# A fused attention and two-mixture kernel: the second mixture's relu is issued earlier in each step, and two integer additions change engine

## The chip, the cores and the metric

The kernel runs on one core of one Trainium2 chip. The metric is device time in microseconds (us) of one execution. Before the change the median of 3 runs is 1346.58 us (1345.78 to 1347.17).

## The reference

The input goes through three stages. Gated linear attention over 4 batches of 8 heads (768 positions, 48 columns) gives x, 3072 tokens of 384 columns. The first mixture ("moe") puts them through a hidden layer of 2048 with a rational gate, the second ("moe2") through four experts with a hidden layer of 1024 and a relu:

```python
def _moe_ref(x, w_in, w_out, a, b):
    h = x @ w_in
    h2 = h * h
    h3 = h2 * h
    P = a[0] + a[1] * h + a[2] * h2 + a[3] * h3
    Q = 1.0 + np.abs(b[0]) * np.abs(h) + np.abs(b[1]) * h2
    g = P / (Q + 1e-06)
    return (g @ w_out).astype(np.float32)

def _moe2_ref(x, domain_probs, w1, w2):
    N, D = x.shape
    E = w1.shape[0]
    p = domain_probs / (domain_probs.sum(-1, keepdims=True) + 1e-09)
    out = np.zeros((N, D), dtype=np.float32)
    for e in range(E):
        h = np.maximum(x @ w1[e], 0.0)
        out += p[:, e:e + 1] * (h @ w2[e])
    return out.astype(np.float32)
```

## The kernel before, in words

Sequence positions are cut into 6 chunks of 128; a chunk is 512 tokens (4 batches). Almost all products are done in a split form: an operand is kept as a rounded high part (gh, w's first half) and the remainder (gl, w's second half), and three products high·high, high·low, low·high are summed.

**Start (about 0 to 122 us).** `first` runs chunk 0's attention, batch by batch. Beside it `conv` turns the 16 weight slots of the first mixture from 64-bit words into 32-bit floats: two passes on ScalarE (L807, L808), a shift and a merge on VectorE (L810, L811), and an integer addition (L814). Slots 0 to 3 have that addition on VectorE, the other twelve on GpSimd. The slots then feed chunk 0's first mixture (`fill_in` L963, `fill_out` L971).

**Steps (from about 122 us).** The main loop has one step for each v of 192: chunk, expert and hidden tile of the second mixture, counted through. `product_order` fixes what TensorE does in a step, in this order: "in2" of tile v+1 (9 matmuls of 512 columns into a hidden bank, of which there are two, `hb[v % 2]`), "out2" of tile v-1 (9 matmuls), then in some steps "in1" of the next chunk's first mixture (9) and "out1" (36, the output of four gated tiles). Where a step has an "out1", tile v+2's "in2" is moved up into it. TensorE's attention matmuls are spread between these (scores L477, key transposes L493, outputs L501, state updates L544).

Beside TensorE a step does, in program order, which is the order in which ScalarE, VectorE and GpSimd take their instructions:

- `relu(v)`: ScalarE writes gh from the hidden bank (L1034), VectorE then writes gl from bank and gh (L1035). Until both have read the bank, "in2" of tile v+2 can't write it; "out2" of tile v needs both results.
- attention's exponentials and inverses (L431, L452), then `gate_in` and `gate_step`, the rational gate of one first-mixture tile: on ScalarE L980, L984 to L986, L1001, L1002 and L1011, on VectorE L995 to L1026. Inside it also stand the w pass of attention (L437) and `evac2`, which weighs an expert's finished sum with its probability (L1069) for GpSimd to add (L1076).
- the late operations of attention (`ops[REST]`): the scans (L444), newton2 (L468), q_hat (L473, GpSimd), the masks of the scores (L488), the copies L497 and L553, finish (L572).
- the splits of weights that are used for the first time (`split_to`): ScalarE rounds (L867), GpSimd, and VectorE in the first steps, subtracts (L869). `take` asks for these when a weight is used, and each step's end asks for up to four ahead.

`relu(v)` stands at the beginning of step v, behind all late operations and splits of step v-1. Only in steps with an "out1" is `relu(v + 1)` issued inside step v, behind the early "in2".

Of the kernel before, what the change touches and what calls it, by code (L numbers as in the profile page):

```python
# [17 lines left out]
NB, NH, S, D = 4, 8, 768, 48  # L18
# [319 lines left out]
CONV1 = (-5, -4, -3, -3, -1, 0, 1, 2, 3, 4, 5, 6, 7, 8, 9, 10)  # L338
NRAW = 8
PRE = 8  # L340
LAST = NCH * NE * NJ2
# [49 lines left out]
def where2(v):  # L391
    return v // (NE * NJ2), v // NJ2 % NE, v % NJ2
# [362 lines left out]
def fused(ctx, tc, aps, consts, gm, big, dp, prep, flag_op):  # L755


    nc = tc.nc
# [38 lines left out]
    def conv(i, stage):  # L797
        if stage == 0:
            t = spare_pools[i % 3].tile([128, 2 * SW], F32, tag=("o", "s1", "pb")[i % 3], name="t")
            temp[i] = t  # L800
        f = temp[i]
        p, m = f[:, 0:SW], f[:, SW:2 * SW].bitcast(I32)
        pi = p.bitcast(I32)
        words = raw[i].rearrange("p (n w) -> p n w", w=2)
        lo, hi = words[:, :, 0], words[:, :, 1]
        if stage == 0:
            nc.scalar.activation(out=p, in_=hi.bitcast(F32), func=AF.Abs, scale=2.0 ** -112, accum_out=big[:, i:i + 1])  # L807
            nc.scalar.activation(out=m, in_=lo.bitcast(U32), func=AF.Identity, scale=2.0 ** -29)  # L808
        else:
            nc.vector.tensor_scalar(pi, pi, 3, None, ALU.logical_shift_left)  # L810
            nc.vector.scalar_tensor_tensor(out=pi, in0=hi, scalar=-2 ** 31, in1=pi, op0=ALU.bitwise_and, op1=ALU.bitwise_or)  # L811
            w1f[i] = wp.tile([128, SW], F32, tag="w", name="wf")
            eng = nc.vector if CONV1[i] < NB - 6 else nc.gpsimd
            eng.tensor_tensor(out=w1f[i].bitcast(I32), in0=pi, in1=m, op=ALU.add)  # L814
            late.append(partial(nc.sync.dma_start, out=w1s[i], in_=w1f[i]))
            if i % 2:
                late.append(fetch)
# [68 lines left out]
    x2, hps, act1, act2 = {}, {}, {}, {}  # L886
# [10 lines left out]
    def fill_step():  # L897
        if fill["done"] < len(fill["ops"]):
            fill["i"] += 1
            to = len(fill["ops"]) * fill["i"]  # L900
            to = -(-to // fill["n"]) if fill["ceil"] else to // fill["n"]
            while fill["done"] < to:
                fill["done"] += 1
                fill["ops"][fill["done"] - 1]()

    def mm_in(ps, w, x):
        wh, wl = w
        n = 0
        for kk in range(3):
            o = slice(kk * 128, (kk + 1) * 128)  # L910
            for a, b in ((wh, x[:, 0]), (wh, x[:, 1]), (wl, x[:, 0])):
                nc.tensor.matmul(ps, a[:, o], b[:, kk, :], start=(n == 0), stop=(n == 8))  # L912
                n += 1
                fill_step()
# [19 lines left out]
    def run_bounds(v):  # L934

        return (v % NJ2 == 0 or v in groups), ((v + 1) % NJ2 == 0 or v + 1 in groups)

    def emit(item):
        kind, what = item
        ts = take(len(halves(item)))  # L940
        if kind == "pre":
            pass
        elif kind == "in2":
            c = where2(what)[0]
            mm_in(hb[what % 2], ts[0], x2[c])
        elif kind == "in1":
            c, j = what
            mm_in(h1, ts[0], att.x[c])
            gate_queue.append((c, j, h1))
        elif kind == "out2":  # L950
            if what >= LAST - NJ2:
                mm_tokens(ts[0], act2.pop(what), *run_bounds(what))
            else:
                mm_out([(ts[0], act2.pop(what))], *run_bounds(what))
        else:
            c, n = what
            mm_out([(ts[i], act1.pop((c, 4 * n + i))) for i in range(4)], True, True)
        make_ready(state["used"] + R)
# [12 lines left out]
            nc.tensor.matmul(acc[m], w[:, o:o + 128], g, start=(j == 0), stop=(j == NJ1 - 1))  # L971


    gate_queue, gate = [], {}

    def gate_in(u):
        h = u[2]
# [11 lines left out]
    def gate_step(new, old, ops):  # L989
# [34 lines left out]
        if old and old[0]:  # L1024
            gl = g1p.tile([128, 512], F32R, tag="gl", name="gl")
            vec.tensor_tensor(out=gl, in0=q0, in1=gh.bitcast(F32), op=ALU.subtract)  # L1026
            act1[old[:2]] = (gh, gl)


    def relu(v):  # L1030
        h = hb[v % 2]
        gh = g2p.tile([128, 512], F32R, tag="gh", name="gh")
        gl = g2p.tile([128, 512], F32R, tag="gl", name="gl")
        nc.scalar.activation(out=gh, in_=h, func=AF.Relu)  # L1034
        nc.vector.scalar_tensor_tensor(out=gl, in0=h, scalar=0.0, in1=gh.bitcast(F32), op0=ALU.max, op1=ALU.subtract)  # L1035
        act2[v] = (gh, gl)
# [85 lines left out]
    for v in range(-FILL - 6, LAST + 1):  # L1122
        tau = v + FILL
        state["vec"] = -1 <= v < 9
        ops = att.begin(v)
        if tau == -3:
            prep.load()
        if tau == -1:
            prep()
        if tau + 6 <= NB:  # L1130
            att.first(tau + 6, conv_ops(tau), fetch, partial(fill_in, 0, 0, NB - 1))
        run_late()
        store_all()
        items = steps.get(v, [])
        lead = 1 if items and items[0][0] == "in2" and items[0][1] == v + 1 else 0
        fill_run(ops[PA], 9 * lead)
        for item in items[:lead]:
            emit(item)
        if 0 <= v < LAST and v not in act2:
            relu(v)  # L1140
        while sums:
            sums.pop()()
        for f in ops[ACT0]:
            f()
        for u in gate_queue:
            if u[0] and u[:2] not in gate:
                gate[u[:2]] = gate_in(u)
        if 0 <= tau + 1 < NJ1:
            fill_in(tau + 1, (NB - 1) * (tau < 0))
        def outputs():  # L1150
            fill_run(ops[PB], 9 * any(item[0] == "out2" for item in items), True)
            for item in items[lead:]:
                if item[0] == "out2":
                    emit(item)
                    if run_bounds(v - 1)[1]:
                        evac2(v - 1)

        amid = 0 < v < LAST and run_bounds(v - 1)[1]
        if v - 1 in groups and groups[v - 1][1]:
            ops[ACT1].append(partial(evac1, *groups[v - 1]))  # L1160
        if amid:
            ops[ACT1].append(outputs)
        ready = [u for u in gate_queue if u[:2] in gate]
        new = ready[0] if ready else None
        if new:
            gate_queue.remove(new)
        old, pend_old = pend_old, new
        if new or old:
            gate_step(new, old, ops)
        else:  # L1170
            for f in ops[DVE1] + ops[ACT1] + ops[POOL1]:
                f()
        c, k = v // (NE * NJ2) - 1, v % (NE * NJ2)
        if v in (LAST - 4, LAST - 3):
            for b in range(2):
                write_out(NCH - 1, b + 2 * (v - LAST + 4), banks[6 + b])
        if 0 <= c < NCH - 1 and k == 2:
            for b in range(2):
                write_out(c, b + (2 if c else 0), banks[6 + b])
        if not amid:  # L1180
            outputs()
        for item in items[lead:]:
            if item[0] == "in2":
                emit(item)
                if v + 1 < LAST:
                    relu(v + 1)
        if 0 <= c < NCH - 1 and k == (1 if c else 2):
            for b in range(2):
                write_out(c, b + (0 if c else 2), banks[6 + b])
        for kind in ("pre", "in1", "out1"):  # L1190
            for item in items[lead:]:
                if item[0] == kind:
                    emit(item)
        for u in gate_queue:
            if not u[0] and u[:2] not in gate:
                gate[u[:2]] = gate_in(u)
        if tau == 0:
            spread_probs()
        if 0 <= tau < NB:
            att.blocks[0, tau].scale_state()  # L1200
        if 0 <= tau - 2 < NJ1:
            fill_out(tau - 2)
        for f in ops[REST]:
            f()
        if v in groups and not groups[v][1]:
            evac1(*groups[v])
        if tau + 6 > NB:
            for f in sum(conv_ops(tau), []):
                f()
            run_late()  # L1210
        if 10 <= tau and v < -1:
            make_ready(min(R - 6, 2 * (tau - 9)))
            split_to(min(AHEAD, state["ready"] - 2))
        if tau == NJ1 + 1:
            for m in range(3):
                split_x2(0, m, acc[m], nc.vector)
            load_pb(0)
        for f in ops[POST]:
            f()
        if v >= -1:  # L1220
            split_to(min(state["used"] + AHEAD, state["split"] + 4))
        att.loads(v)
        if v == 170:
            flag_op(banks[6], banks[7])
# [180 lines left out]
```

## Time and profile before

| | us |
|---|---|
| median of 3 runs | 1346.58 |
| profiled execution, its own time | 1346.18 |
| its span (first to last instruction) | 1344.30 |
| TensorE matmuls busy | 1321.2 |
| TensorE weight loads busy | 1058.5 |
| VectorE busy | 888.9 |
| ScalarE busy | 682.1 |
| GpSimd busy | 277.4 |

The mean granted TensorE clock is 0.999 of full speed. Engines run side by side, so the busy times don't add up to the span. A matmul's end in the profile is modelled, and consecutive matmuls overlap; where one engine waits, the row of the instruction behind the wait says so in brackets, with the instruction that ended it.

### The profile page before, as it was taken

Reading aid. Unit: us, or ns where it says so; the run is one execution under the profiler, and the core shown is the slowest. Engines: PE = TensorE matmul, PEld = TensorE weight load, DVE = VectorE, ACT = ScalarE, POOL = GpSimd, SP = SyncE. Lnnn points to the kernel's source line nnn. Section 1 sums busy time; section 2 is a strip of 40 time slices with the busy share of each in tenths; the row PEclk is TensorE's granted clock in tenths of the full one; section 3 lists DMA queues with packets and bytes.
Section 4 is the critical chain, followed back from the end, with each engine's and each line's share of the span. In section 5 each row is a group of like instructions: output and inputs, shape, how many; then the busy total and the mean of one; then the engine's idle time right before and its main releaser. Section 6 shows DMA issues by size and latency. Waiting matters only on the chain.

```text
span 1344.3 us, 19607 instructions
## 1 busy us (share of the span) xinstructions
PE 1321.2 (98%) x7180; PEld 1058.5 (79%) x7180; DVE 888.9 (66%) x1366; ACT 682.1 (51%) x1188; POOL 277.4 (21%) x234
## 2 busy tenths in 40 slices
PE   8999999999999999999999999999999999999998
PEld 8445888777788888888888888888888888888887
DVE  7998868998566666767575847575756565752221
ACT  6997568767265545345554525554525444421111
POOL 2333344576410022101020220010210010110010
PEclk9999999999999999999999999999999999999999
DMA  9538985777785666676666657656757666667660
GB/s 344 212 143 308 377 316 200 276 246 269 273 273 187 190 199 188 186 260 200 200 216 186 207 189 251 213 186 199 227 175 240 194 191 196 191 192 242 196 189 27
DMA packets 116856, 294.17 MB, mean 219 GB/s; under 512 B 13232, under 2 KB 28944, under 8 KB 115984
## 3 DMA queue, kind: packets, MB, share of 16 engines
q1 hardware_dynamic: 116320, 292.70, 65.7%
q8 instruction: 59, 0.97, 0.3%
q14 instruction: 45, 0.37, 0.1%
q10 hardware_dynamic: 432, 0.13, 0.0%
HBM read 243.98 MB, written 48.81 MB: 218 GB/s over the span
## 4 chain that ended last, share of the span: by engine, by line


## 5 line engine op out<-in xcount | busy, mean ns | idle before, releaser
L912 PE MATMUL bank<-x,w 128*128 128x512 f32 x2448 | 593.3, 391 | 6.3 <-DVE gl L1035 5.5
L912 PEld LDWEIGHTS bank<-x,w 128*128 128x128 f32 x2448 | 457.1, 188 | 103.3 <-DVE gl L1035 6.9
L922 PE MATMUL bank<-gh,w 128*128 128x512 f32 x1584 | 492.7, 392 | 2.0 <-ACT gh L1011 1.2
L922 PEld LDWEIGHTS bank<-gh,w 128*128 128x128 f32 x1584 | 294.0, 188 | 67.9 <-issue 4.0
L922 PE MATMUL bank<-gl,w 128*128 128x512 f32 x792 | 308.6, 390 | 0.0
L1035 DVE SCALAR_TENSOR_TENSOR gl<-bank,gh 128x512 fp32r<-128x512 f32 x192 | 131.7, 686 | 137.6 <-ACT gh L1034 137.2
L1076 POOL TENSOR_TENSOR o<-o,t 128x512 f32<-128x512 f32 x64 | 92.4, 1470 | 534.7 <-DVE t L1069 534.7
L1034 ACT ACTIVATE gh<-bank 128x512 fp32r<-128x512 f32 x192 | 113.7, 593 | 120.0 <-PE bank L912 120.0
L922 PEld LDWEIGHTS bank<-gl,w 128*128 128x128 f32 x792 | 148.7, 188 | 31.2
L1000 DVE SCALAR_TENSOR_TENSOR q<-q,sc,r 128x512 f32<-128x512 f32 x80 | 63.4, 793 | 142.3 <-ACT r L985 142.3
L1011 ACT CAST gh<-q 128x512 fp32r<-128x512 f32 x80 | 49.2, 615 | 163.0 <-DVE q L1009 162.8
L980 ACT COPY h<-bank 128x512 f32<-128x512 f32 x80 | 47.0, 588 | 117.5 <-PE bank L912 117.4
L1026 DVE TENSOR_TENSOR gl<-q,gh 128x512 fp32r<-128x512 f32 x80 | 58.3, 729 | 51.7 <-ACT gh L1011 51.7
L869 POOL TENSOR_TENSOR w<-rawbuf,w 128x384 fp32r<-128x384 f32 x68 | 80.1, 1204 | 32.2 <-ACT w L867 25.0
L1021 DVE SCALAR_TENSOR_TENSOR y<-y,sc,h 128x512 f32<-128x512 f32 x80 | 74.8, 935 | 2.8
L1001 ACT ACTIVATE r<-q,sc 128x512 f32<-128x512 f32 x80 | 58.0, 725 | 23.2 <-DVE q L1000 16.3
L995 DVE SCALAR_TENSOR_TENSOR q<-q,r 128x512 f32<-128x512 f32 x80 | 69.2, 864 | 0.1
L458 POOL TENSOR_TENSOR k<-k,g 112x512 f32<-112x512 f32 x23 | 34.4, 1498 | 156.3 <-DVE g L444 93.3
L986 ACT ACTIVATE y<-h,sc 128x512 f32<-128x512 f32 x80 | 64.2, 802 | 0.0
L1009 DVE SCALAR_TENSOR_TENSOR q<-y,sc,q 128x512 f32<-128x512 f32 x80 | 62.2, 778 | 1.8
L1093 DVE TENSOR_TENSOR s<-s,bank 128x512 f32<-128x512 f32 x45 | 30.0, 684 | 49.4 <-PE bank L922 49.4
L1002 ACT ACTIVATE r<-r 128x512 f32<-128x512 f32 x96 | 60.7, 633 | 3.0
(117 smaller groups left out, 1273.3 us busy)
## 6 DMA issues: line engine op xcount, KB each, us to landing
w<-ws SPq DMA_DIRECT2D x456, 384.0 KB, 3.5
ws<-w SPq DMA_DIRECT2D x96, 384.0 KB, 5.1
raw<-in_w_dram SPq DMA_DIRECT2D x16, 768.0 KB, 6.9
rawbuf<-in_w_dram SPq DMA_DIRECT2D x64, 192.0 KB, 4.7
v<-in_v_dram SPq DMA_DIRECT2D x24, 320.0 KB, 5.0
f<-in_qkf_dram SPq DMA_DIRECT2D x24, 256.0 KB, 4.2
k<-in_qkf_dram SPq DMA_DIRECT2D x24, 256.0 KB, 4.4
q<-in_qkf_dram SPq DMA_DIRECT2D x24, 256.0 KB, 4.5
```

Source lines behind the costliest of these rows:

```text
L869: eng.tensor_tensor(out=t[:, 1], in0=r, in1=t[:, 0].bitcast(F32), op=ALU.subtract)
L912: nc.tensor.matmul(ps, a[:, o], b[:, kk, :], start=(n == 0), stop=(n == 8))
L922: nc.tensor.matmul(acc[m], a[:, o], b, start=(start and n == 0), stop=(stop and n == last))
L986: nc.scalar.activation(out=y, in_=h, func=AF.Identity, scale=sc[:, 0:1], bias=sc[:, 1:2])
L995: vec.scalar_tensor_tensor(out=q0, in0=q0, scalar=QC, in1=r0, op0=ALU.add, op1=ALU.mult)
L1000: vec.scalar_tensor_tensor(out=q, in0=q, scalar=sc[:, 5:6], in1=r, op0=ALU.mult, op1=ALU.add)
L1002: nc.scalar.activation(out=r, in_=r, func=AF.Exp, scale=-1.0)
L1009: vec.scalar_tensor_tensor(out=q0, in0=y0, scalar=sc[:, 3:4], in1=q0, op0=ALU.subtract, op1=ALU.mult)
L1021: vec.scalar_tensor_tensor(out=y, in0=y, scalar=sc[:, 2:3], in1=h, op0=ALU.subtract, op1=ALU.mult)
L1034: nc.scalar.activation(out=gh, in_=h, func=AF.Relu)
L1035: nc.vector.scalar_tensor_tensor(out=gl, in0=h, scalar=0.0, in1=gh.bitcast(F32), op0=ALU.max, op1=ALU.subtract)
L1076: add()
```

## The change

Two edits. The additions of slots 2 and 3 in `conv` go from VectorE to GpSimd. And a new `relu_next(v)` issues the relu of tile v+1 inside step v, right behind the gate step, if its "in2" is already issued; the call at a step's beginning stays, but finds every tile done. `filled` keeps the tiles whose "in2" is issued. TensorE's order and SyncE's (the DMA queue) are the same before and after; ScalarE's and VectorE's change.

```diff
-            eng = nc.vector if CONV1[i] < NB - 6 else nc.gpsimd
+            eng = nc.vector if i < 2 else nc.gpsimd
...
             mm_in(hb[what % 2], ts[0], x2[c])
+            filled.add(what)
...
-    gate_queue, gate = [], {}
+    gate_queue, gate, filled = [], {}, set()
...
+    def relu_next(v):
+        if 0 <= v + 1 < LAST and v + 1 in filled and v + 1 not in act2:
+            relu(v + 1)
...
             for f in ops[DVE1] + ops[ACT1] + ops[POOL1]:
                 f()
+        relu_next(v)
         c, k = v // (NE * NJ2) - 1, v % (NE * NJ2)
...
             if item[0] == "in2":
                 emit(item)
-                if v + 1 < LAST:
-                    relu(v + 1)
+                relu_next(v)
```

VectorE where the steps begin (end of step -1 to the first scans of step 0; bank_88 and bank_89 are the two hidden banks, so the L1035 rows are the relus of tiles 0 and 1, which stand at L1040 in the changed file), before:

```order
L473 TENSOR_TENSOR q<-q,i 112x512
L869 TENSOR_TENSOR w<-rawbuf,w 128x384 x3
L1035 SCALAR_TENSOR_TENSOR gl<-bank_88,gh 128x512
L488 TENSOR_TENSOR am_1215<-bank_90,mask 128x512
L488 TENSOR_TENSOR am_1217<-bank_92,mask 128x512
L444 SCALAR_TENSOR_TENSOR g<-f,sc 112x128 x4
L869 TENSOR_TENSOR w<-rawbuf,w 128x384 x2
L1035 SCALAR_TENSOR_TENSOR gl<-bank_89,gh 128x512
```

and with the change:

```order
L473 TENSOR_TENSOR q<-q,i 112x512
L869 TENSOR_TENSOR w<-rawbuf,w 128x384
L1040 SCALAR_TENSOR_TENSOR gl<-bank_88,gh 128x512
L869 TENSOR_TENSOR w<-rawbuf,w 128x384 x2
L1040 SCALAR_TENSOR_TENSOR gl<-bank_89,gh 128x512
L488 TENSOR_TENSOR am_1219<-bank_90,mask 128x512
L488 TENSOR_TENSOR am_1221<-bank_92,mask 128x512
L444 SCALAR_TENSOR_TENSOR g<-f,sc 112x128 x4
```

Tile 0's relu passes two subtractions of splits; tile 1's passes two masks, four scans and two subtractions.

VectorE from the gate's end in step 21 (L1026) to the gate of step 22; the L1035 row is the relu of tile 22. Before:

```order
L1021 SCALAR_TENSOR_TENSOR y<-y,sc,h 128x512
L1026 TENSOR_TENSOR gl<-q,gh 128x512
L444 SCALAR_TENSOR_TENSOR g<-bank_92,sc 112x128 x4
L1035 SCALAR_TENSOR_TENSOR gl<-bank_88,gh 128x512
L995 SCALAR_TENSOR_TENSOR q<-q,r 128x512
```

and with the change:

```order
L1022 SCALAR_TENSOR_TENSOR y<-y,sc,h 128x512
L1027 TENSOR_TENSOR gl<-q,gh 128x512
L1040 SCALAR_TENSOR_TENSOR gl<-bank_88,gh 128x512
L444 SCALAR_TENSOR_TENSOR g<-bank_92,sc 112x128 x4
L996 SCALAR_TENSOR_TENSOR q<-q,r 128x512
```

The relu now stands ahead of the four scans; all else keeps its place. The same happens with the scans at the ends of steps 15, 27, 35 and of others later.

VectorE from step 38's gate (L1026) to that of step 39, around the masks of a chunk-3 block; the L1035 row is the relu of tile 39. Before:

```order
L1026 TENSOR_TENSOR gl<-q,gh 128x512
L488 TENSOR_TENSOR am_3987<-bank_91,mask 128x512
L488 TENSOR_TENSOR am_3989<-bank_92,mask 128x512
L1035 SCALAR_TENSOR_TENSOR gl<-bank_89,gh 128x512
L995 SCALAR_TENSOR_TENSOR q<-q,r 128x512
```

and with the change:

```order
L1027 TENSOR_TENSOR gl<-q,gh 128x512
L1040 SCALAR_TENSOR_TENSOR gl<-bank_89,gh 128x512
L488 TENSOR_TENSOR am_3991<-bank_91,mask 128x512
L488 TENSOR_TENSOR am_3993<-bank_92,mask 128x512
L996 SCALAR_TENSOR_TENSOR q<-q,r 128x512
```

The two masks now stand behind the relu.

## Rows read from the trace of the kernel before

**Rows 1.** Page, part 1: busy time, share of the span and instructions of each engine.
```profile
PE 1321.2 (98%) x7180; PEld 1058.5 (79%) x7180; DVE 888.9 (66%) x1366; ACT 682.1 (51%) x1188; POOL 277.4 (21%) x234
```

**Rows 2.** Busy us of each engine (x instructions), PEclk, DMA share and GB/s, by windows.
```profile
200.00:300.00 100.00, 97.00 (x553) 78.78 (x552) 93.22 (x118) 71.46 (x132) 58.89 (x47) 1.00 0.68 244
300.00:400.00 100.00, 94.64 (x538) 77.44 (x539) 68.63 (x99) 54.01 (x99) 43.29 (x38) 1.00 0.78 270
400.00:500.00 100.00, 99.81 (x580) 81.88 (x579) 68.79 (x108) 51.12 (x87) 12.61 (x11) 1.00 0.61 196
```

**Rows 3.** Waits of PE, whole span: us in total, times, longest us.
```profile
PE bank L912 <- DVE gl L1035: 5.5, 4, 1.8
...
PE bank L493 <- DVE am L488: 1.1, 2, 0.9
```

**Rows 4.** Start, timeline 0 to 60: start us, us, engine, line, [idle before].
```profile
32.78 0.96 DVE L814 CUSTOM_DVE_ANT_0 wf<-t 128x1536 uint16<-128x1536 uint16 x1
...
32.82 2.11 PE L963 MATMUL bank<-x,wf 128*128 128x384 f32 x6
33.66 1.28 DVE L488 TENSOR_TENSOR am<-bank,mask 128x512 f32<-128x512 f32 x2
...
34.99 0.81 PEld L501 LDWEIGHTS bank<-am,v 128*32 128x32 f32 x32 [0.68 <-DVE am L488]
```

**Rows 5.** Groups by line, whole span: xcount | busy us, mean ns | idle before.
```profile
L1035 DVE SCALAR_TENSOR_TENSOR gl<-bank,gh 128x512 fp32r<-128x512 f32 x192 | 131.7, 686 | 137.6 <-ACT gh L1034 137.2
...
L995 DVE SCALAR_TENSOR_TENSOR q<-q,r 128x512 f32<-128x512 f32 x80 | 69.2, 864 | 0.1
...
L814 POOL TENSOR_TENSOR wf<-t 128x768 int32<-128x768 int32 x12 | 21.9, 1827 | 47.6 <-DVE t L811 44.6 <-ACT r L985 3.0
...
L995 DVE SCALAR_TENSOR_TENSOR bank<-bank,r 128x512 f32<-128x512 f32 x16 | 11.1, 694 | 0.1
```

**Rows 6.** Timeline 126 to 129.5, relu of tile 0.
```profile
126.25 1.49 DVE L869 TENSOR_TENSOR w<-rawbuf,w 128x384 fp32r<-128x384 f32 x3
...
127.65 0.68 DVE L1035 SCALAR_TENSOR_TENSOR gl<-bank,gh 128x512 fp32r<-128x512 f32 x1
...
128.39 1.45 PE L912 MATMUL bank<-x,w 128*128 128x512 f32 x5 [0.77 <-DVE gl L1035]
```

**Rows 7.** Timeline, scans at the end of step 15, and the first op of step 17's gate.
```profile
223.13 0.58 ACT L1034 ACTIVATE gh<-bank 128x512 fp32r<-128x512 f32 x1
223.29 1.37 DVE L444 TENSOR_TENSOR_SCAN g<-bank,sc 112x128 f32<-112x128 f32 x4
...
243.45 1.01 DVE L1000 SCALAR_TENSOR_TENSOR q<-q,sc,r 128x512 f32<-128x512 f32 x1 [0.42 <-ACT r L985]
```

**Rows 8.** Timeline 283 to 296.5, scans of step 21 and what follows.
```profile
283.93 1.36 DVE L444 TENSOR_TENSOR_SCAN g<-bank,sc 112x128 f32<-112x128 f32 x4
285.32 0.60 ACT L452 ACTIVATE bank<-g 112x512 f32<-112x512 f32 x1 [4.03 <-DVE g L444]
...
288.35 0.75 DVE L1000 SCALAR_TENSOR_TENSOR q<-q,sc,r 128x512 f32<-128x512 f32 x1 [0.18 <-ACT r L985]
...
293.54 2.38 DVE L995 SCALAR_TENSOR_TENSOR q<-q,r 128x512 f32<-128x512 f32 x1
```

**Rows 9.** Timeline 334 to 345, relu of tile 29, the last that TensorE waits for.
```profile
342.57 0.68 DVE L468 SCALAR_TENSOR_TENSOR i<-i,bank 112x512 f32<-112x512 f32 x1
...
344.02 1.19 PE L912 MATMUL bank<-x,w 128*128 128x512 f32 x4 [1.76 <-DVE gl L1035]
```

**Rows 10.** Timeline 385.5 to 409.5, scans of step 35, masks of step 38.
```profile
387.03 0.58 ACT L1034 ACTIVATE gh<-bank 128x512 fp32r<-128x512 f32 x1
387.12 1.37 DVE L444 TENSOR_TENSOR_SCAN g<-bank,sc 112x128 f32<-112x128 f32 x4 [0.60 <-ACT bank L437]
...
407.36 1.28 DVE L488 TENSOR_TENSOR am<-bank,mask 128x512 f32<-128x512 f32 x2
...
408.10 0.60 PE L493 MATMUL bank<-ident,k 112*128 112x112 f32 x4 [0.19 <-DVE am L488]
```

## Prediction

> **What bounds the kernel now.** I read the busy times first: TensorE's matmuls cover 1321.2 of 1344.3 us [rows 1], so 23 us of the span are all that any change of the order can free. The windows say where they lie: from 400 us on TensorE is at 99.81 of 100, and between 200 and 400 it lacks 3.00 and 5.36 us [rows 2]. In the first of these two stretches VectorE is at 93.22. There first uses of weights (splits), attention and the gate of chunk 1 all meet, and I take this stretch to be bound by VectorE and ScalarE, not by TensorE; the waits of TensorE are where it catches up with them. The list of waits names the relu first: four times TensorE's "in2" waited for gl, 5.5 us in all, and twice a key transpose waited for the masks, 1.1 us [rows 3]. The change goes at the first kind. Its largest possible gain there is those 5.5 us, 0.4%.
>
> **The two additions.** On VectorE the addition takes 0.96 [rows 4], on GpSimd 1.83 [rows 5]. GpSimd has nothing urgent then and the two slots are needed only later, so its longer time costs nothing; without that cover, one addition's 0.87 would show. The masks behind slot 2's addition could start 0.96 earlier than 33.66. But the outputs L501 behind them stand on TensorE behind L963, which runs from 32.82 for 2.11, to 34.93; the weight load of L501 started at 34.99 after an idle 0.68 [rows 4]. So the gain is at least 0.06 and at most 0.96; since matmul ends are modelled and the next can enter a little earlier, I take 0.2, near the lower end. Slot 3's addition leaves VectorE ahead of work that waits for ScalarE anyway: 0. **-0.2.**
>
> **Tile 0's relu** passes two of three subtractions. The three start at 126.25 and give way to the relu at 127.65, 0.47 each, so it comes 0.93 earlier. TensorE's idle time in front of tile 2's "in2" was 0.77 [rows 6], which goes; masks and scans behind, later by a relu, have over a step until they are needed. **-0.8.** TensorE and all that it feeds enter the dense stretch 1.0 early.
>
> **Steps 15 to 29.** Here I follow VectorE and ScalarE, since TensorE waits for them several times up to its wait at 344.02 [rows 9], which wipes out what it did before. Four places count.
>
> - Step 15: the scans started at 223.29. With the change VectorE takes the relu first, and that waits for its own ScalarE half, which ends at 223.13 + 0.58 = 223.71 [rows 7]; then the relu itself (mean 0.686 [rows 5]; rows of back-to-back ops overlap a little, so I count 0.6). The scans start at about 224.3, 1.0 late, with them the inverse on ScalarE, and behind it in the queue the copy and squares of the next gate. The gate in step 17 had its first op wait 0.42 for ScalarE [rows 7]; ScalarE there hangs on TensorE, which is early, so this takes 0.4 back. Offset: -1.0 + 1.0 - 0.4 = -0.4.
> - Step 21: again the relu goes ahead of the scans at 283.93, without a wait of its own. ScalarE's inverse had waited 4.03 us for the scans, and the gate's first op behind it waited only 0.18 for ScalarE [rows 8]. So the 0.6 passes on whole: +0.2.
> - Steps 27 to 29: the scans of step 27 again wait some 0.4 for a relu's ScalarE half, as in step 15; but tile 29's relu no longer stands behind newton2 (0.68 at 342.57 [rows 9]), which brings TensorE's "in2" 0.6 forward. Offset: 0.0.
> - Tiles 24 and 28: their relus come earlier too, and two of the four waits of [rows 3] shrink. That only lets TensorE run into the next wait on the same chain sooner: it counts nothing. If that cover is missing, it is the first rival.
>
> So of the 1.0 won ahead of 200 us nothing is left at 346 us. Bounds: between the whole 1.0 kept and 1.0 to 1.5 lost, if the 0.4s are not regained.
>
> **Steps 35 to 39** are a second, small place of this kind: chunk 3 starts its gate in four steps running. The scans of step 35 had waited 0.60 for the w pass on ScalarE and started at 387.12; behind the change VectorE waits for a relu whose ScalarE half ended at 387.03 + 0.58 = 387.61, and runs it, 1.1 in all [rows 10]. ScalarE has one relu less in front of that, so I take 0.6 (bounds 0 to 1.1). From there VectorE has no idle time down to the masks of step 38 (407.36), which now stand behind tile 39's relu, 0.6 more; the key transpose behind them already waited [rows 10]. **+1.2** (0 to 1.7). Behind this, TensorE is at 99.81 with masks and scans that have more than a step to spare; the same reordering in the later chunks costs 0.
>
> **Sum.** -0.2 - 0.8 + 1.0 (lost again) + 1.2 = +1.2. The profiled execution took 1346.18, giving 1347.4; it lies 0.4 under the median of the runs, 1346.58, and against that the forecast is **1347.8**. Less than 0.2%, 2.7 us, can't be told from no change here, so the forecast is "the same".
>
> [...] The relu on VectorE keeps to 0.686 in the mean beside a busy GpSimd, while the gate's L995, which reads two operands outside PSUM, has a mean of 0.864, against 0.694 in its form on a bank [rows 5], and 2.38 at 293.54 [rows 8]. So some relus now run in time that a gate op would lose. [...]
>
> **Rivals.**
>
> 1. The relu's waits go for good. If VectorE's queue is not the bound and only its order was, all of 5.5 [rows 3] goes, and the start's 0.2: 1340.9. For it: the relu is named in four of the waits. Against: VectorE at 93.22 [rows 2] has hardly any idle time in which work could be done earlier. 12%.
> 2. The delays behind are hidden: chains at steps 15, 21 and 35 have more slack than I see, and the early 1.0 stays: 1345.6. For it: each delay is only 0.6 to 1.0, and the scans' users are a step away; against: waits of 0.18 [rows 8] and 0.19 [rows 10] that are already at the edge. 30%.
> 3. Slower: the gate's ops take the relus' place beside GpSimd's splits. One such meeting cost 2.38 - 0.69 = 1.7 at 293.54 [rows 8]. If two more of that size come about between 220 and 345 us, where the splits run, the time is 1347.8 + 3.4 = 1351.2. It decides from one such meeting on (1349.5). For it: GpSimd is at 58.89 of 100 there [rows 2]; against: as many meetings may close as open. 13%.
>
> The forecast has the remaining 45%, with about 1.2 us to either side. That no relu moves in time, because ScalarE or VectorE would wait for TensorE in both orders, is true of most steps after 410 us and is part of the forecast.
>
> **Numbers.** Faster by over 0.2% needs 1343.9 or less: the first rival and a little of the second, 0.16. Slower needs 1349.3 or more: the third and the edge of the forecast, 0.14. The rest, 0.70, is within 0.2%. The range goes from 1343.2, short of the first rival's 1340.9, to 1350.0, short of the third's 1351.2; it leaves out some 2 in 10.
>
> **What would show it.** Right: the wait of "in2" for the relu gone or nearly gone at about 127, TensorE's waits for the masks grown from 1.1 to about 2, the scans of step 15 and 35 starting about 1 and 0.6 later against TensorE, the wait before tile 31's "in2" still there, and windows from 450 on without a change. Wrong: a list of waits without any relu and a shorter total between 200 and 400 (first rival), or VectorE's mean of L995, L997 and L1009 clearly above before's (third).

## The result and the profile after

The changed kernel takes 1352.9 us (median; 1352.47 to 1355.71), the kernel before, beside it, 1345.7. The ratio is 1.0052, 95% interval [1.0042, 1.0062]: 7.0 us slower, outside the range of the forecast. The profiled execution of after took 1352.52, its span is 1350.3. In after's file the lines stand a few further down: L995 is L996, L997 L998, L1000 L1001, L1004 L1005, L1009 L1010, L1011 L1012, L980 L981, L1035 L1040; lines under 900 keep their numbers.

The page of after, part 1:

```profile
PE 1324.9 (98%) x7180; PEld 1060.3 (79%) x7180; DVE 897.4 (66%) x1364; ACT 681.6 (50%) x1188; POOL 283.8 (21%) x236
```

VectorE has two instructions less than in [rows 1] and is busy 8.5 us longer. The gate's ops make it: those that read two operands outside PSUM (560 ops on the eight lines L996, L998, L1001, L1005, L1010, L1020, L1022 and L1027) take 464.3 us together, in before 455.4. The windows of after (as in [rows 2]; the column behind POOL is PEclk, TensorE's granted clock) say where TensorE lost:

```profile
200.00:300.00 100.00, 96.77 (x546) 78.44 (x545) 94.96 (x117) 69.25 (x126) 56.92 (x46) 0.98 0.67 234
300.00:400.00 100.00, 92.92 (x524) 75.44 (x523) 66.76 (x95) 53.26 (x98) 43.48 (x38) 0.98 0.78 269
400.00:500.00 100.00, 98.60 (x574) 80.87 (x573) 71.79 (x111) 50.74 (x87) 14.99 (x12) 1.00 0.63 197
```

TensorE does seven matmuls less in the first hundred and fourteen less in the second, and PEclk is 0.98 where it was 1.00. Two things were lost, then: time in which TensorE waits, and clock. The waits of PE in after (us in total, times, longest us):

```profile
PE bank L912 <- DVE gl L1040: 4.6, 3, 2.4
...
PE bank L912 <- ACT h L981: 3.1, 2, 2.3
...
PE bank L922 <- ACT gh L1012: 2.5, 1, 2.5
PE bank L493 <- DVE am L488: 1.4, 1, 1.4
```

The wait for the relu is still the largest: 4.6 instead of 5.5 [rows 3], but 2.4 at a time. New are 2.3 for h and 2.5 for gh (0.8 and 1.2 before). Both belong to chunk 1's gate: h is ScalarE's copy of the first mixture's hidden bank, which frees the bank for TensorE, and gh the rounded high part of the gate's result. Windows of after around the two longest of them that were followed by a slower clock:

```profile
248.00:251.00 3.00, 1.38 (x7) 0.79 (x5) 2.96 (x5) 2.97 (x6) 0.15 (x1) 1.00 1.03 414
251.73:255.14 3.41, 3.41 (x8) 2.73 (x9) 3.38 (x5) 2.56 (x4) 1.52 (x2) 0.50 1.03 413
...
347.30:350.71 3.41, 3.41 (x9) 2.66 (x9) 2.68 (x5) 0.18 (x1) 3.04 (x3) 0.50 0.10 41
352.00:355.00 3.00, 3.00 (x15) 2.48 (x14) 0.69 (x1) 0.00 (x0) 2.64 (x3) 1.00 1.01 293
```

Behind each of these two waits TensorE does 8 or 9 matmuls in 3.41 us at a granted clock of 0.50, where at 1.00 it does 15 in 3.00. Before's profile shows no such stretch between 10 and 1341 us.

Taking the start of each block of matmuls in after and before gives this ledger, in us of after's lateness. It enters "in2" of tile 0 at -0.63, gains 0.84 with tile 0's relu, and has lost 0.61 of that by 168 us. At "in1" of chunk 1's tile 8 (251.72) it loses 2.8, mainly the wait for h; by tile 20's "in2" another 1.7 (half clock); then 1.2 and 0.7 come back, since waits that before had there are gone. At 317.8 it loses 1.0 (gh), at 350.8 1.8 (mainly half clock), at 417.0 1.2 (masks), near 845 and 1256 another 0.6 together. The end is 6.4 late.

What makes h late? VectorE's timeline in after, around step 17's gate:

```profile
237.44 7.67 DVE L996 SCALAR_TENSOR_TENSOR q<-q,r 128x512 f32<-128x512 f32 x1
245.14 1.39 DVE L998 SCALAR_TENSOR_TENSOR q<-q,r 128x512 f32<-128x512 f32 x1
246.46 1.48 DVE L1001 SCALAR_TENSOR_TENSOR q<-q,sc,r 128x512 f32<-128x512 f32 x1
```

and GpSimd's:

```profile
237.43 3.93 POOL L869 TENSOR_TENSOR w<-rawbuf,w 128x384 fp32r<-128x384 f32 x4
241.31 1.30 POOL L473 TENSOR_TENSOR q<-q,i 112x512 f32<-112x512 f32 x1
242.56 4.84 POOL L869 TENSOR_TENSOR w<-rawbuf,w 128x384 fp32r<-128x384 f32 x4
```

The same place in before, VectorE and then GpSimd:

```profile
236.87 3.50 DVE L995 SCALAR_TENSOR_TENSOR q<-q,r 128x512 f32<-128x512 f32 x1
240.40 2.62 DVE L997 SCALAR_TENSOR_TENSOR q<-q,r 128x512 f32<-128x512 f32 x1
...
236.87 4.38 POOL L869 TENSOR_TENSOR w<-rawbuf,w 128x384 fp32r<-128x384 f32 x4
```

In both kernels VectorE's op and GpSimd's first split begin together. The same op has a mean of 0.83 (0.86 before), and here it ends inside GpSimd's fourth instruction from there on (before, at 240.37) or its eighth (after, at 245.11). VectorE's next wait for ScalarE, 0.42 in [rows 7], is gone, because VectorE itself is now the late one: L1001 starts at 246.46 instead of 243.45, and h follows.

One thing is not alike, on ScalarE: the four casts that feed GpSimd's next splits. They stand behind copies of a bank that TensorE fills, so they keep TensorE's time and not VectorE's. Before:

```profile
239.90 1.75 ACT L867 CAST w<-rawbuf 128x384 fp32r<-128x384 f32 x4
```

and after:

```profile
239.35 1.75 ACT L867 CAST w<-rawbuf 128x384 fp32r<-128x384 f32 x4
```

Against the start of VectorE's op that is 3.03 us in before and 1.91 in after, where VectorE is later and TensorE earlier.

### The profile page after: what moved, and what is told of

The parts are those of the page before. It is cut to its first block, busy times and chain, and to the rows that moved or that the text cites. A ratio compares the mean times of both kernels' runs of the same rounds, so it can differ in the third digit from the quotient of the medians.

```text
span 1350.3 us, 19568 instructions
## 1 busy us (share of the span) xinstructions
PE 1324.9 (98%) x7180; PEld 1060.3 (79%) x7180; DVE 897.4 (66%) x1364; ACT 681.6 (50%) x1188; POOL 283.8 (21%) x236
## 4 chain that ended last, share of the span: by engine, by line
## 5 line engine op out<-in xcount | busy, mean ns | idle before, releaser
L1040 DVE SCALAR_TENSOR_TENSOR gl<-bank,gh 128x512 fp32r<-128x512 f32 x192 | 131.7, 686 | 123.5 <-ACT gh L1039 123.1
L1001 DVE SCALAR_TENSOR_TENSOR q<-q,sc,r 128x512 f32<-128x512 f32 x80 | 66.5, 832 | 158.2 <-ACT r L986 158.2
L1012 ACT CAST gh<-q 128x512 fp32r<-128x512 f32 x80 | 49.2, 615 | 159.4 <-DVE q L1010 159.2
L981 ACT COPY h<-bank 128x512 f32<-128x512 f32 x80 | 47.1, 588 | 113.2 <-PE bank L912 113.2
L1027 DVE TENSOR_TENSOR gl<-q,gh 128x512 fp32r<-128x512 f32 x80 | 57.4, 718 | 51.7 <-ACT gh L1012 51.7
L1022 DVE SCALAR_TENSOR_TENSOR y<-y,sc,h 128x512 f32<-128x512 f32 x80 | 74.1, 927 | 2.8
L996 DVE SCALAR_TENSOR_TENSOR q<-q,r 128x512 f32<-128x512 f32 x80 | 66.4, 830 | 0.2
L1010 DVE SCALAR_TENSOR_TENSOR q<-y,sc,q 128x512 f32<-128x512 f32 x80 | 62.8, 785 | 1.8
L1074 DVE TENSOR_TENSOR t<-bank,pb 128x512 f32<-128x512 f32 x69 | 46.7, 690 | 25.4 <-PE bank L922 24.1
```

The lines of the kernel that those rows point to most:

```text
L996: vec.scalar_tensor_tensor(out=q0, in0=q0, scalar=QC, in1=r0, op0=ALU.add, op1=ALU.mult)
L1001: vec.scalar_tensor_tensor(out=q, in0=q, scalar=sc[:, 5:6], in1=r, op0=ALU.mult, op1=ALU.add)
L1010: vec.scalar_tensor_tensor(out=q0, in0=y0, scalar=sc[:, 3:4], in1=q0, op0=ALU.subtract, op1=ALU.mult)
L1022: vec.scalar_tensor_tensor(out=y, in0=y, scalar=sc[:, 2:3], in1=h, op0=ALU.subtract, op1=ALU.mult)
```

## The experiments

Three theories stood after the result. **Sequence:** the moved relus make scans and masks late, and these delays add up. **Meetings:** a moved relu changes which gate ops run into GpSimd's splits (L996 above); the waits that follow cost TensorE clock as well. **Additions:** the other entry alone shifts it all. Nearly every kernel is after with one line ahead of the new call in step v, so that the relus of the steps that the line leaves out stand where before has them. "The base" is the kernel only_to_8. A ratio of 1.0010 is 1.35 us.

### Which edit, and which steps

**adds_only**, before with the additions alone:
```diff
-            eng = nc.vector if CONV1[i] < NB - 6 else nc.gpsimd
+            eng = nc.vector if i < 2 else nc.gpsimd
```


> The kernel before with the two additions on GpSimd alone; no relu moves. Sequence theory (the relus delay scans and masks, and the delays add up) and meeting theory (a moved relu shifts VectorE against GpSimd's splits, so that one gate operation of step 17 loses 7.67 instead of 3.50 us, and TensorE's clock falls behind the long wait): both expect the 0.63 us by which tile 0's in2 came earlier, and no more: 1345.0 to 1345.7. Additions theory (it is the 0.6 us earlier entry that shifts VectorE against GpSimd): the loss is here, +2 to +6 us on before, 1347.5 to 1352.

Measured: 1345.5 (ratio 0.9992 [0.9983, 1.0001]). The additions theory falls.

**relu_only**, after with the additions back on VectorE:
```diff
-            eng = nc.vector if i < 2 else nc.gpsimd
+            eng = nc.vector if CONV1[i] < NB - 6 else nc.gpsimd
```


> The kernel after with the two additions back on VectorE: only the relus move. Sequence theory: after's time plus 0.6, 1353.5. Meeting theory: the relus are the cause, so 1350 to 1354, but the entry 0.6 us later may change which operation meets a split, so a value between 1346 and 1350 would speak for meetings and against a fixed sum. Additions theory: no loss is left, 1344.5 to 1345.7.

Measured: 1354.9, ratio 1.0056 [1.0043, 1.0070]. The relus are the whole loss, and the op of step 17 takes 7.66 here too.

**only_to_8**, early relus in steps 0 to 8 only, and **ends_only**, in all but steps 9 to 39:
```diff
+        if v < 9:              # only_to_8
+        if v < 9 or v >= 40:   # ends_only
             relu_next(v)
```


> The additions, and the relu early only in steps 0 to 8; from step 9 on the order of before. Sequence theory: no scan or mask is delayed, so the 0.6 and the 0.8 us won ahead of 130 us are kept or absorbed: 1344.2 to 1345.7. Meeting theory: the same, unless the entry 1.4 us earlier into the stretch from 200 to 350 us brings a meeting by itself: then 1347 to 1350.

> The additions and every early relu but those of steps 9 to 39. All theories that put the loss between 200 and 420 us: as the kernel with early relus in steps 0 to 8 alone, within 0.6 us (TensorE's shifts of +0.23 near 845 and +0.57 near 1256 us in the kernel after stay): 1345.5 to 1347. If the many relus moved after 420 us cost more than the trace shows: over 1348.

Measured: 0.9999 [0.9990, 1.0008] and 1.0001 [0.9992, 1.0009]. So the whole loss comes from steps 9 to 39, and no step outside them gains anything measurable.

### Which order: VectorE's or ScalarE's

**act_half**: from step 9 on only ScalarE's half of the relu is early; VectorE's order is before's. `relu` is cut in two for it, and `relu_high` issues ScalarE's half.
```diff
-        relu_next(v)
+        relu_next(v, v >= 9)
...
-            relu(v + 1)
+            (relu_high if high else relu)(v + 1)
```


> The kernel after, but from step 9 on only ScalarE's half of the next relu is taken behind the gate; VectorE's half stands where before has it. The relu on ScalarE now goes ahead of the casts L867 on which GpSimd's splits wait, but VectorE's order is that of before. ScalarE theory (the casts and with them GpSimd's splits move by a relu, 0.58 us, and that sets which gate operations meet them): as after, 1350 to 1354. VectorE theory (its own order makes the delays: scans and masks behind a relu): as the kernel with early relus in steps 0 to 8 alone, 1345 to 1346.5, or less, since the relu's high half is there sooner.

Measured: 1347.9, ratio 1.0018 [1.0009, 1.0027]. Between the two: ScalarE's order alone costs about 2.4 us, VectorE's the larger rest. On ScalarE the relu stands ahead of casts L867 that come later for it; that this is what costs the 2.4 is not shown.

**not_15_17**, **scans_first**, **masks_first**, **both_first**: the old place in some steps.
```diff
+        if v not in (15, 16, 17):                           # not_15_17
+        if v not in (9, 15, 21, 27, 35):                    # scans_first
+        if v not in (12, 18, 30, 38):                       # masks_first
+        if v not in (9, 12, 15, 18, 21, 27, 30, 35, 38):    # both_first
             relu_next(v)
```


> The kernel after, but the relus of tiles 16 to 18 are taken where before took them (on VectorE that puts one relu, tile 16's in step 15, behind the scans again). Meeting theory: the gate operation of 7.67 us in step 17 is back at about 3.5, TensorE's wait of 2.50 us before chunk 1's in1 8 is under 1, its clock stays up there, and the time falls by 2.3 us (what the stretch from 249 to 279 us lost on balance) or more, if what follows from the shift at 280 to 350 us goes as well (another 2.8): 1347.8 to 1350.6. Sequence theory: only the scans of step 15 come earlier, by 1.0 us: 1351.9.

> The kernel after, but in the steps whose attention takes scans (9, 15, 21, 27, 35) the relu stays behind them as before. Sequence theory: the scans' 1.0 + 0.6 + 0.6 + 0.6 us are not lost, and what tiles 24 and 28 win is kept: 1349.5 to 1350.5. Meeting theory: VectorE's phase against the splits is another; not a fixed sum, but the 7.67 us operation goes, as it did where steps 15 to 17 were undone, and other long ones may come: 1348 to 1353.

> The kernel after, but in the steps whose attention takes masks (12, 18, 30, 38) the relu stays behind them as before. Both theories: the wait of 1.4 us for the masks in front of the key transpose near 414 us shrinks by one relu, 0.6 to 0.7 us; nothing else, so 1352.0 to 1352.5; less by 1 to 2 us only if the relu ahead of the masks of step 18 makes part of the loss near 255 us.

> The kernel after with the old place in both kinds of steps: relus pass only splits, casts and other late operations. Sequence theory: no scan and no mask is later than before, so the gains are left alone: 1343 to 1345.5. Meeting theory: ScalarE's casts still stand behind a relu, so a part of the loss stays: 1347 to 1351.

Measured, with three columns from the traces: the time from step 15's first output matmul to step 21's (some 219 to 280 us), step 17's first gate op, and the stretches at half clock between 200 and 1330 us in the one profile of each kernel.

| kernel | ratio [95%] | step 15 to 21 | gate op | half clock |
|---|---|---|---|---|
| before | 1 | 60.70 | 3.50 | 0 |
| after | 1.0052 [1.0042, 1.0062] | 63.37 | 7.67 | 2 |
| relu_only | 1.0056 [1.0043, 1.0070] | 63.21 | 7.66 | 1 |
| not_15_17 | 1.0044 [1.0031, 1.0058] | 63.68 | 3.50 | 2 |
| masks_first | 1.0046 [1.0032, 1.0060] | 62.99 | 7.66 | 3 |
| scans_first | 1.0033 [1.0021, 1.0045] | 62.87 | 3.51 | 1 |
| both_first | 1.0013 [1.0004, 1.0022] | 61.12 | 3.50 | 1 |
| act_half | 1.0018 [1.0009, 1.0027] | 61.79 | 3.50 | 1 |
| only_15 | 1.0015 [1.0007, 1.0024] | 62.95 | 7.66 | 2 |
| only_18 | 1.0002 [0.9993, 1.0010] | 61.06 | 3.50 | 0 |

Undoing the scans gives back 2.6 us, the masks 0.8 (not told apart from 0), both 5.3. By their times not_15_17 (1352.7) falls to the sequence theory and both_first (1348.4) to the meetings. The 7.67 us op goes with the scans of step 15, as the meeting theory wants, but that doesn't heal the stretch: in not_15_17 another wait grows in its place. Its waits of PE:

```profile
PE bank L912 <- DVE gl L1040: 3.4, 2, 1.9
PE bank L493 <- DVE am L488: 3.3, 2, 2.1
PE bank L922 <- ACT gh L1012: 2.5, 1, 2.5
```

The key transpose L493 now waits 2.1 for the masks of step 18, which stand behind tile 19's relu, and half clock follows it. So neither theory is enough alone: in this stretch VectorE has no slack, and whichever of its products TensorE needs next becomes the wait.

The long op is not the only meeting. The time of the 560 gate ops together tells of all of them: 464.3 us in after, 463.2 in relu_only, 462.3 in masks_first, 461.5 in not_15_17, 461.1 in act_half, 460.7 in scans_first and 459.8 in both_first, and 455.4 to 457.7 in before and all other kernels. So early relus in many of the steps 9 to 39 lengthen the gate's ops by 2 to 9 us, with the 7.67 us op or without it. How much of that TensorE feels is not a fixed share: act_half and scans_first lie 0.4 apart here and 2.0 in time.

### One step at a time

**only_15**, **only_18**, **only_21_28**, **only_35_39**: the base and these steps alone.
```diff
+        if v < 9 or v == 15:              # only_15
+        if v < 9 or v == 18:              # only_18
+        if v < 9 or v in (21, 27, 28):    # only_21_28
+        if v < 9 or 35 <= v <= 39:        # only_35_39
             relu_next(v)
```


> Additions, early relus in steps 0 to 8, and tile 16's in step 15, ahead of the scans. If the moved scans are enough by themselves: the gate operation of 7.67 us in step 17 and a wait of over 2 us before chunk 1's in1 8, 1347.5 to 1349.5. By the forecast's term (scans 1.0 late, 0.4 regained) the step adds 1.0 to in2 of tile 20 at most: 1345.5 to 1347.

> The same with tile 19's relu in step 18, ahead of the masks, alone. If the masks are enough by themselves: TensorE's wait for them near 256 us grows from 0.92 to 1.5, no drop of the clock, later waits shrink by it: 1345.5 to 1346.6. If only scans and masks together make waits of over 2 us: the same; a wait of over 2 us there, or over 1347.5, would say that one relu alone is enough.

> Additions, steps 0 to 8, and the relus taken early in steps 21, 27 (ahead of scans) and 28 (ahead of the second Newton step). By the forecast's terms: +0.6 in step 21, +0.6 - 0.6 and another -0.2 in steps 27 to 29, so 1346.0 to 1347.0. If each delay is followed by longer waits and a clock drop as in the kernel after (wait of 2.38 us, then half clock at 347): 1348 to 1350.

> Additions, steps 0 to 8, and the relus taken early in steps 35 to 39. By the forecast's term (scans +0.6, masks +0.6; +1.24 in the kernel after): the wait of 1.4 us for the masks near 412 us, and 1346.8 to 1347.6. If the term only exists in a kernel that comes there with VectorE late: 1345.7 to 1346.3.

**only_15** measured 1348.1, ratio 1.0015 [1.0007, 1.0024]: one relu ahead of four scans costs some 2 us. VectorE and GpSimd in its trace:

```profile
237.94 7.66 DVE L996 SCALAR_TENSOR_TENSOR q<-q,r 128x512 f32<-128x512 f32 x1
...
237.93 3.93 POOL L869 TENSOR_TENSOR w<-rawbuf,w 128x384 fp32r<-128x384 f32 x4
241.81 1.29 POOL L473 TENSOR_TENSOR q<-q,i 112x512 f32<-112x512 f32 x1
243.06 4.82 POOL L869 TENSOR_TENSOR w<-rawbuf,w 128x384 fp32r<-128x384 f32 x4
```

TensorE's wait for h is 2.2 and half clock follows at 253.1. Over all profiles, before's included, the op took 7.66 or 7.67 in each of the four kernels that have tile 16's relu ahead of step 15's scans (after, relu_only, masks_first, only_15) and 3.49 to 3.51 in each of the other fourteen. That the moved relu makes it is shown; why the op ends in GpSimd's fourth instruction in the one order and in its eighth in the other is not. ScalarE's casts part the two groups without an exception: they start 1.91 to 2.02 us behind the op's start in the four kernels and 2.25 to 3.04 behind it in the fourteen. That earlier casts are the cause, by giving GpSimd its next splits in time, is not tested.

**only_18**: 1.0002 [0.9993, 1.0010], the masks' wait grows to 1.5 and no clock is lost: one relu ahead of masks is free there. **only_21_28**: 1.0010 [1.0001, 1.0018], about 1.4; in its trace the wait in front of tile 31's "in2" is 2.35. **only_35_39**: 1.0012 [1.0004, 1.0021], about 1.6; the masks' wait is there as in after:

```profile
PE bank L493 <- DVE am L488: 2.2, 2, 1.4
```

Above the base the four make 2.2 + 0.4 + 1.5 + 1.8 = 5.9, of the 7.1 that after lies above it. With intervals of 1.2 us to either side of each part the two can't be told apart. The 2.4 of act_half is no further part, since these kernels move ScalarE's half as well.

**pick_24_29**: the base and the two relus that pass neither scans nor masks and that TensorE waited for.
```diff
+        if v < 9 or v in (23, 28):
             relu_next(v)
```


> The additions, early relus in steps 0 to 8, and from there on only the two that neither pass scans nor masks and whose tiles 24 and 29 TensorE waited for before (1.79 and 1.76 us). If the waits on a relu are worth anything by themselves: 0.9 us off at tile 26's in2 and some 1 us off at tile 31's, 1344.0 to 1345.3. If VectorE's and ScalarE's chain is the bound and TensorE runs into the next wait: 1345.5 to 1347.

Measured: 1.0002 [0.9993, 1.0010]. Its waits of PE:

```profile
PE bank L922 <- ACT gh L1012: 2.5, 1, 2.5
PE bank L912 <- DVE gl L1040: 2.2, 3, 0.9
```

The relu's waits fall from 5.5 [rows 3], 4.7 with tile 0's gone, to 2.2, and the total stays: the wait for the gate's gh at 314 us, behind tile 26's "in2" at 299, grows from 1.2 to 2.5, and in this profile half clock follows it at 315. TensorE arrives earlier at a chain that is not earlier.

### What the clock costs

**wait_1** and **wait_3**: before, with VectorE's half of five late relus repeated, so that TensorE waits where all else is quiet.
```diff
+        for _ in range(10 if v in (165, 172, 175, 178, 181) else 1):   # wait_3: 13
             nc.vector.scalar_tensor_tensor(out=gl, in0=h, ...
```


> The kernel before; VectorE's half of the relu is done ten times instead of once for five late tiles (165, 172, 175, 178, 181), where TensorE had no wait and in2 two tiles on had 4.60 us to spare. Nine more of 0.62 us are 5.6: five isolated waits of TensorE of about 1.0 us, no drop of its granted clock behind them, 5.0 us in all: 1351.

> The same with thirteen: five waits of about 2.8 us, 14.2 us in all. If waits of that size make TensorE's granted clock fall, as behind the waits of 2.34 and 2.38 us in the kernel after: half clock for 3.41 us behind some or all of them, at about 1.6 us each, 14.2 + 1.6 to 8.0: 1361.5 to 1368. If the drops there had another cause: 1360 and the clock at full.

Measured: 1357.9 (1.0083 [1.0069, 1.0098]) and 1377.5 (1.0238 [1.0223, 1.0253]). I had the waits too small: a repeated op starts every 0.73 us, not 0.62, and the waits are 1.82 to 1.87 and 3.99 to 4.05. In wait_1 half clock follows the waits at 1277 and 1308 and not the other three. The third wait in its timeline:

```profile
1277.41 0.96 PE L912 MATMUL bank<-x,w 128*128 128x512 f32 x3 [1.87 <-DVE gl L1036]
```

and the windows behind it:

```profile
1278.31:1281.72 3.41, 3.41 (x10) 2.64 (x9) 0.00 (x0) 0.60 (x1) 0.00 (x0) 0.50 0.00 0
1282.00:1285.00 3.00, 3.00 (x15) 2.48 (x14) 2.66 (x4) 0.00 (x0) 2.11 (x2) 1.00 0.46 146
```

Each wait makes TensorE 1.95 to 2.16 late, and each of the two with half clock another 1.7. In wait_3 half clock follows all five and they cost 6.3 each on average, more than 2 above the wait itself. So the clock is a term of its own, and it is not fixed: the same wait may or may not be followed, and what decides that is not shown.

## Why the prediction was wrong

Point by point, by its own steps.

- **What bounds the kernel**: right. VectorE is the bound of the stretch from 200 to 300 us (94.96 of 100 now), and pick_24_29 shows that TensorE's waits on the relu are where it catches up with that chain. The first rival is out.
- **The additions, -0.2**: not to be seen. "in2" of tile 0 starts at 121.78 with them and at 121.77 without; over the kernels with both edits it lies between 120.7 and 123.4, so the -0.63 of after's profile is no more than this spread.
- **Tile 0's relu, -0.8**: right, 0.84, and the wait of 0.77 [rows 6] is gone. That it lasts until 200 us was not: 0.61 is lost again by 168 us, in ends_only and only_to_8 as well.
- **Step 15, 1.0 - 0.4**: the scans start at 223.89 in after, with TensorE 0.7 to 0.9 early, so they are 1.3 to 1.5 late against it: right in kind. **What failed is that the sum has no term for the gate's ops beside GpSimd's splits**; only the third rival prices them. Over the 560 gate ops they came out at 464.3 - 455.4 = 8.9 us more of VectorE, 7.0 of them between about 190 and 415 us. The meeting that is shown to cost time by itself stands right behind step 15, where the trace of before already showed 3.50 and 2.62 us for two ops with means of 0.86 and 1.06 (the row of step 17 that I took showed only the op behind them, [rows 7]). only_15 measures the step at some 2 us, where I had 0.6 lost and none after it.
- **Steps 21 to 29**: +0.4 over these steps in the forecast, 1.4 measured alone (0.1 to 2.4), so not told apart; in after, with all other early relus, TensorE's lateness grows by 2.8 between 283 and 359 us. The wait before tile 31's "in2" is there as foretold, but it grew from 1.76 [rows 9] to 2.38.
- **Steps 35 to 39, +1.2**: right in sum, and partly by luck. TensorE loses 1.24 there in after and 1.33 with these steps alone, with the masks' wait at 1.40. But the split into 0.6 for the scans and 0.6 for the masks doesn't come out: scans_first, whose scans of step 35 stand first again, waits 1.40 too, and masks_first, whose scans are late, 0.65, where the kernels with before's order here wait 0 to 0.55.
- **The clock** has no term in the forecast. The two stretches at half clock make TensorE 1.7 and 1.6 later, some 3.3 of the 9.1 us that the ledger loses behind 168 us, before 1.9 come back. Most of the first comes back where before waits anyway: relu_only has the same op and a wait of 2.24 for h, no half clock behind it, and its step 15 to 21 takes 63.21, after's 63.37.
- **Later chunks, 0**: 0.2 near 845 and 0.3 near 1256 us in after, but nothing measurable in ends_only.
- **The third rival** named the loss, longer gate ops beside GpSimd's splits, with a price of 1.7 for one meeting and 13%. The longest meeting is 4.2 us longer than before's, of which the op behind it gives 1.2 back (2.62 to 1.39), and this one place was enough for some 2 us. The sign I gave came half true: the mean of L995 fell from 0.864 [rows 5] to 0.830, since the long op of [rows 8] at 293.54 is 0.68 now, while that of L997 rose from 1.061 to 1.200 and that of L1009 from 0.778 to 0.785 (L1004, which I didn't name, rose from 0.790 to 0.917). That one op of L995 went from 3.50 to 7.67 only the timeline shows.

The gate's ops set beside the relu: in all profiles, every VectorE instruction of over 2 us between 100 and 460 us is a gate op with two operands outside PSUM. The longest of them lasts 7.67, while the 192 relus, which read one operand from a bank, lie between 0.66 and 0.70 in before and in after. What makes the one kind long and not the other is not shown.

## What to carry over

In a stretch where VectorE is as full as here (93 to 95 of 100), moving work earlier for one consumer made another late. Before taking a wait away, read which product of the same engine TensorE needs next and how much slack that has; two waits of 1.8 us there were worth nothing. Look through the timeline for the longest single instructions of a kind, not at the mean of one line alone: here an op at four times its mean marked a place where one relu of 0.6 us moved ahead cost some 2 us. And where all else is quiet, five TensorE waits of some 4.0 us, each with half clock behind it, cost 6.3 each (wait_3), so several short waits may be better than one long; that is an estimate from the counts below and not tried.

No version here beats the kernel before by more than can be measured; the additions alone (0.9992 [0.9983, 1.0001]) are the nearest.

## What the runs showed of the hardware

- In step 17 VectorE's first gate op, with two operands outside PSUM (0.83 in the mean in after), began with a GpSimd split and ended inside GpSimd's fourth instruction from there on (3.50 us, before) or its eighth (7.67 us, after). The splits that lie wholly within the op took 1.01 to 1.03 on GpSimd, those begun within it or behind it, beside the next gate ops, 1.45 to 1.48.
- The granted clock fell behind waits well inside a busy stretch. Over all eighteen profiles, between 200 and 1330 us, none of the 78 waits of 0.6 to 1.7 us went with half clock from about its end (0.4 us ahead of it to 1.5 behind); 8 of 27 between 1.7 and 2.0 did, 11 of 18 between 2.0 and 2.6, and all five of 4.0. Each time it was at 0.50 for 3.41 us, in wait_3 twice for 6.82. The kernel before isn't free of it: wait_1 and wait_3, which are the kernel before until 1200 us, show it behind the 1.80 wait at 301 us, where before's own profile doesn't.
